# Spreading GpSimd's gathers and scatters over the steps of an attention and the phases of a mixture of experts

## The chip, the cores and the metric

The kernel runs on one core of a Trainium2 chip. The metric is device time in microseconds (us) of one execution. The engines named below are TensorE (PE; its weight loads are shown apart as PEld), VectorE (DVE), ScalarE (ACT), GpSimd (POOL) and SyncE (SP, which only issues DMAs here). Each runs its own stream of instructions in order; between engines, semaphores order the work.

## The reference

Two blocks follow each other: an attention over chunks (4 batches, 8 heads, 768 positions, head dimension 64), and a feed-forward of 8 experts in which each of the 3072 tokens goes to one expert.

```python
for c in range(S // 32):                      # chunks of 32 queries
    q_c   = q[:, :, 32*c : 32*c + 32]
    ctx   = positions max(0, 32*c - 16) .. min(S, 32*c + 40)
    k_full, v_full = [mem_k | k[ctx]], [mem_v | v[ctx]]      # 8 memory rows ahead
    a = softmax(q_c @ k_full.T / sqrt(64))
    out[:, :, chunk] = a @ v_full
x = out.transpose(0, 2, 1, 3).reshape(3072, 512)
logits = x @ w_gate                           # 8 experts
e = argmax(logits);  gate = softmax(logits)[e]
y = gate * (relu(x @ w1[e]) @ w2[e])          # w1[e]: 512 x 1024, w2[e]: 1024 x 512
```

All of it is 32-bit floating point.

## The kernel before

**Attention.** The queries are cut into 32 blocks (`NB`) of 96, three chunks each. One loop, `for i in range(NB + 3)`, holds a software pipeline whose order is written out by hand: step i turns q or k of a later block on PE (L623), computes the scores of block i (L662), takes their exponential on ACT in three instructions (L675), multiplies the exponentials of block i-1 with v (`values`, L686), divides on DVE (L689, L691), turns the result of block i-2 (`turn_xb`, L696, copied by ACT) and computes the gate's logits of block i-3 (L710). SP loads q, k and v some blocks ahead, and from step 6 a quarter of a weight matrix every third step (`fetch_w`). `values` writes its 96 x 528 rows into one of 13 slots of the tile `big`; besides 512 values of x a row holds the gate and the token's number.

**Routing.** Blocks are routed in seven groups, (0,6), (6,12), (12,17), (17,22), (22,27), (27,30), (30,32). Two steps after a group's end `choose` takes the argmax (GpSimd counts the tokens seen of each expert); a step later `label` writes gate and token number into the rows; a step later `rank` works out, with two matmuls and DVE, the row `dest` of each token in a DRAM buffer that is sorted by experts. Then `scatter` (L773) sends each block's 96 rows of 2112 bytes there, an indirect DMA that GpSimd issues. The program has two of them a step. They need only `dest` and the rows; nothing else holds them back.

**Early work.** After group 3, at step 29, GpSimd gathers (L825) the first 256 tokens of expert 0 into `xe2`, followed by a `drain` of its engine; PE turns them (L863) at step 31 and starts their first layer (`early_first`, L869).

**Transition.** After the loop come the last scatters of the group before, `choose` and `label` of the last group, its `rank`, `count_up` (how many tokens each expert has, and the rows to gather), the last two scatters, three memsets on DVE (L1286), the second layer of the early tokens (L1292), and between its halves the gathers of expert 0's and expert 1's tokens, four indirect DMAs of 128 rows each (`fetch_x`).

**Experts.** For each expert `lead` issues three products ahead, then a `Switch` on the number of its tokens takes one of 65 cases. Its width is that number's half, rounded up; an expert too large for one pass is done in two parts (here expert 4). Both layers are matrix products by a scheme of seven products instead of eight (`product`, L1116), which needs sums of quarters of the weights (`sum_weights`, L1092, four of them a layer, DVE) and of x (`sums`, `sum4`). `first_layer` goes through phases: P1 with P2, P6, P7, P5, P4, P3. In each PE makes two products into banks of PSUM, and DVE adds them (L1157, L1165, L1169, L1174, L1176, L1180, L1189), with ReLU on ACT (L1145). Woven in between are the last expert's results, which are turned (`turn_y`, L1039), multiplied by the gate on ACT (L1044) and stored by an indirect DMA (`put_back`, L1050), and the turning of the next expert's x (`turn_x`, L1033, copied by ACT at L1034). GpSimd's program in an expert is: four gathers for expert e + 2 at the beginning, then the four stores. The weight sums for the second layer stand after P7 (two), after P5 (one) and at the end (one). `second_layer` has the same products, with `between` (sums of x and of the next weights) after the first.

Of the kernel before, what the change touches and what calls it, by code (L numbers as in the profile page):

```python
# [24 lines left out]
NB = B * NQB  # L25
# [485 lines left out]
def ordinary(ctx, tc, q, k, v, mem_k, mem_v, moe_w_gate, moe_w1, moe_w2, out, good):  # L511
# [144 lines left out]
    def scores(i):  # L656
        s, (b, qb) = st[i], divmod(i, NQB)
        w0 = window(qb)
        p0 = QB // 2 * (i % 2)
        sc = ps_s.tile([128, H, 128], F32, tag="s", name="sc")  # L660
        for a in range(H // 2):
            mm(  # L662
                sc[:, 2 * a : 2 * a + 2, 0:QB].rearrange("p x (j t) -> p x j t", j=2),
                lhsT=turned[b][:, a, w0 : w0 + WIN],
                rhs=units[i // 2]["qT"][:, a, :, :, p0 : p0 + QB // 2],
                start=True,
                stop=True,
            )
        ex = s["ex"] = apool.tile([128, H, QB], F32, name="ex")
        x = 0 if qb == 0 else 2 if qb == NQB - 1 else 1  # L670
        sc4 = sc[:, :, 0:QB].rearrange("p h (j t) -> p h j t", j=2)
        ex4 = ex.rearrange("p h (j t) -> p h j t", j=2)
        for g in range(3):
            sl = slice(CHUNK // 2 * g, CHUNK // 2 * g + CHUNK // 2)
            nc.scalar.activation(  # L675
                ex4[:, :, :, sl], sc4[:, :, :, sl], AF.Exp, bias=mask[:, 3 * x + g : 3 * x + g + 1], scale=D**-0.5
            )

    def values(i, g, bank):
        s = st[i]  # L680
        if g == 0:
            s["x"] = xr[:, i % NXR, 0:DM]
        o = bank[0:QB, 0 : 4 * (D + 1)].rearrange("p (h d) -> p h d", h=4)
        for j in range(4):
            h = 4 * g + j
            mm(o[:, j], lhsT=s["ex"][:, h], rhs=s["v"][:, h], start=True, stop=True)  # L686

        inv = inv_all[:, i, 4 * g : 4 * g + 4]
        nc.vector.reciprocal(inv, o[:, :, D])  # L689
        x = s["x"].rearrange("p (h d) -> p h d", h=H)  # L690
        nc.vector.tensor_tensor(x[:, 4 * g : 4 * g + 4], o[:, :, 0:D], bc(inv, 2, D), op=OP.mult)  # L691
    def turn_xb(i):
        s = st[i]
        tx = ps_t.tile([128, DM // 128, QB], F32, tag="t", name="tx")
# [73 lines left out]

    scatters = []

    def scatter(t0, t1):
        for t in range(t0, t1):
            i = nc.gpsimd.indirect_dma_start(  # L773
                out=x_dram,
                out_offset=bass.IndirectOffsetOnAxis(ap=dest[:, t : t + 1], axis=0),
                in_=xr[:, t % NXR].bitcast(I32),
                in_offset=None,
                bounds_check=E * XC - 1,
                oob_is_err=False,
            )  # L780
            for j in scatters:
                tc.declare_no_dep(i.ins, j, reason="rows of different tokens")
            scatters.append(i.ins.name)

    def wait_for(i, name):
        tc.add_manual_dep(
# [33 lines left out]

        return rows_of

    def gather(to, which):
        after_scatters(
            nc.gpsimd.indirect_dma_start(  # L825
                out=to.bitcast(I32),
                out_offset=None,
                in_=x_dram,
                in_offset=bass.IndirectOffsetOnAxis(ap=which, axis=0),
                bounds_check=E * XC - 1,  # L830
                oob_is_err=False,
            )
        )

    def need(i, f):
        if 0 <= i < NB:
# [35 lines left out]
    with tc.manual_schedule():  # L872
# [8 lines left out]
        for name, u in ((turn_k, 0), (turn_q, 0), (turn_k, 1)):  # L881
            name(u, 0)
            name(u, 1)
            if name is turn_q:
                turn_mem()
                place_mem(0)
        for i in range(NB + 3):

            u = i // 2 + 1 + i % 2
# [6 lines left out]
            if u < NU:  # L896
                f(u, 0)
            need(i, scores)
            banks = [ps_o.tile([128, 512], F32, tag="o", name="o") for _ in range(2)]
            then = []  # L900
            for g in range(last):
# [10 lines left out]
                values(i - 1, 1, banks[1])  # L912
            if late:
                nc.vector.tensor_copy(*late)
            for f2 in then:
                f2()
            clear(i)
            if u < NU:
                f(u, 1)
            for g in range(last):  # L920
                if i == GROUPS[g][1] + 2:
                    choose(g)
                if i == GROUPS[g][1] + 3:
                    label(g)

            for g in range(last):
                for j in range(2 * (i - GROUPS[g][1] - 4), 2 * (i - GROUPS[g][1] - 4) + 2):
                    t = GROUPS[g][0] + j
                    if GROUPS[g][0] <= t < GROUPS[g][1]:
                        scatter(t, t + 1)  # L930
                        sent = t + 1
            if i == EARLY + 7:
                for g in range(2):
                    gather(xe2[:, g], rows0[:, g : g + 1])
                nc.gpsimd.drain()
            if i == NB - 1:
                early_turn()
            if i >= NB:
# [81 lines left out]
        nc.vector.tensor_scalar(most[:, 0:1], most[:, 0:1], float(XC), None, op0=OP.is_le)  # L1020
        nc.vector.tensor_tensor(good, most[0:1, 0:1], most[0:1, 1:2], op=OP.mult)

    def fetch_x(to, e, k):


        nc.gpsimd.memset(to[:, :, DM].bitcast(I32), SKIP)
        for g in range(4):
            gather(to[:, g], rows[:, e, 2 * k + g // 2, g % 2 : g % 2 + 1])

    def turn_x(x, g):  # L1030
        tx = tiles[g % 2]
# [104 lines left out]
        product(1, banks[2], w, a, 2)  # L1136
        return [turn_y(yTs[(e - 1) % 2], g) for g in (2, 3)] if e else []

    def first_layer(e, hf, backs, turns, new):


        a = halves(xT, KX, hf)
        w, a = weights(e, 0), streams(a, xS[:, :, :, 0:hf])
# [11 lines left out]
        for p in range(2):  # L1155
# [3 lines left out]
                for n in range(4):  # L1159
                    fetch_w(e + 1, 0, n, after=i)  # L1160
            relu(to(0, 0, p))
        for f in backs[:2]:
            f()
        for p in range(2):
            add(T(p), T(p), P(6, p), op=OP.add)  # L1165
        for f in backs[2:]:
            f()
        for p in range(2):
            add(T(2 + p), T(p), P(7, p), op=OP.add)  # L1169
        if new:  # L1170
            sum_weights(e, 1, (5, 6))
        for p in range(2):
            p5 = P(5, p)
            add(to(1, 1, p), T(2 + p), p5, op=OP.add)  # L1174
            relu(to(1, 1, p))
            add(T(p), T(p), p5, op=OP.add)  # L1176
        if new:
            sum_weights(e, 1, (4,))
        for p in range(2):
            add(to(1, 0, p), T(2 + p), P(4, p), op=OP.add)  # L1180
            relu(to(1, 0, p))
        for f in turns[:1]:
            f()
        for p in range(2):
            sums(hh, s, C(p))
            p3 = P(3, p)
            for f in turns[1:2] if p == 0 else turns[2:]:
                f()
            add(to(0, 1, p), T(p), p3, op=OP.add)  # L1189
            relu(to(0, 1, p))  # L1190
        for p in range(2):
            sum4(hh, s, C(p))
        if new:
            sum_weights(e, 1, (7,))

    def second_layer(e, hf, yT, between, last):
        w, a = weights(e, 1), streams(halves(h, KH, hf), hS[:, :, :, 0:hf])
        p1, u2, u3 = (tmp[:, i, :, 0:hf] for i in (0, 4, 5))
        P = lambda i, b: product(i, banks[b], w, a, 0)
        nc.scalar.copy(p1, P(1, 2))  # L1200
        between()
        p4, p5 = P(4, 3), P(5, 4)
        add(u2, p1, P(6, 0), op=OP.add)
        add(u3, u2, P(7, 1), op=OP.add)
        add(yT[:, 2:4, 1, 0:hf], u3, p5, op=OP.add)
        add(u2, u2, p5, op=OP.add)
        add(yT[:, 0:2, 1, 0:hf], u3, p4, op=OP.add)
        add(yT[:, 0:2, 0, 0:hf], p1, P(2, 2), op=OP.add)
        if e + 1 == E and last:
            end_half(yT, tgs[e % 2])  # L1210
        P(3, 5)
# [9 lines left out]
    def expert(e, n, ty):  # L1221
# [8 lines left out]
            backs = [lambda g=g: put_back(*args, g, ty[g - 2]) for g in (2, 3)] + both(put_back, *args)[:2]  # L1230
        yT = yTs[e % 2]
        x = xes[e % 2]
        if len(ps) == 2:
            fetch_x(xe2, e, 1)
        for k, w in enumerate(ps or [0]):
            last = k + 1 >= len(ps)
            tg = tgs[e % 2 if last else 2]
            nc.vector.tensor_copy(tg, x[:, :, DM : DM + 2])
            if k == 0 and e + 2 < E:
                fetch_x(x, e + 2, 0)  # L1240
            x = xes[(e + 1) % 2] if last else xe2
            turns = both(turn_x, x) if not last or e + 1 < E else []
            if w:
                first_layer(e, w // 2, backs, turns, k == 0)
            else:
                for f in backs + turns:
                    f()
                if e + 1 < E:
                    for i in range(4):
                        fetch_w(e + 1, 0, i)  # L1250
# [8 lines left out]
                    sum_weights(e + 1, 0)  # L1259

            if w:
                second_layer(e, w // 2, yT, between, last)
            else:
                between()
                if e + 1 == E:
                    end_half(yT, tg)
            if not last:
# [4 lines left out]
        return {eng.engine: eng.value_load(cases[0:1, c : c + 1], min_val=0, max_val=n - 1) for eng in engines}  # L1272

    with tc.manual_schedule():
        scatter(sent, GROUPS[last][0])
        choose(last)
        label(last)

        for f in range(6, KH):
            early_first(f, banks[f - 2][:, 0])  # L1280
            if f == 6:
                rank(last, banks[2].rearrange("p a b -> p (a b)"))()
                count_up(banks[3])
                scatter(GROUPS[last][0], NB)
        for t in [xes[1]] + yTs:
            nc.vector.memset(t, 0.0)  # L1286
        w2 = ws[0][1].rearrange("p (k n) -> p k n", n=DM)
        engines = (nc.tensor, nc.scalar, nc.vector, nc.gpsimd, nc.sync)
        for g in range(2):
# [1 line left out]
            for f in range(KH):  # L1291
                mm(py, lhsT=h0[:, f, 128 * g : 128 * g + 128], rhs=w2[:, f], start=f == 0, stop=f == KH - 1)  # L1292
            if g == 0:
                fetch_x(xes[0], 0, 0)
                fetch_x(xes[1], 1, 0)
                sum_weights(0, 0)
                index = [loads(engines, e, CASES) for e in range(E)]
                in_range = nc.values_load(good[0:1, 0:1], min_val=0, max_val=1)
                for g2 in range(4):
                    turn_x(xes[0], g2)  # L1300
                sums_of_x()
# [55 lines left out]
```

## Time and profile before

| | |
|---|---|
| median of 3 runs | 599.84 us (596.56 to 600.42) |
| profiled execution | 601.19 us, span 599.4 us |
| mean granted clock of PE | 0.957 |
| busy: PE, DVE, ACT, POOL | 537.7, 323.1, 175.9, 133.6 us |
| chain that ended last | PE 73%, DVE 11%, issue 4%, ACT 4%, another core or an unknown queue 4%, DMA 4% |
| L773 scatters | 32, median 922 ns each |
| L825 gathers | 38, median 1007 ns each |
| L1050 stores by `tg` | 32, mean 1027 ns each |
| L1092 weight sums | 1.22 us each |

The span is the time between the first and the last instruction of the profiled execution; the time of that execution has some 1.8 us more around it. Busy time is the sum of an engine's instructions; for PE it contains the time that they take longer at a lower clock. The granted clock is 1.00 where PE runs at full speed. The chain is followed back from the last instruction to what released each; "another core or an unknown queue" stands for a wait whose end the profile can't put down to a finished instruction or transfer (it is printed as "remote" in the list of waits). A line of a timeline gives start, duration, engine, line of the kernel, operation, output and inputs, and in square brackets how long the engine had been idle and what ended that.

### The profile page before, as it was taken

To read this page: it belongs to the slowest core of one execution; us is meant where nothing else is said; L and a number is where in the kernel's file an instruction comes from. 1 tells how busy PE (TensorE), PEld (TensorE's weight loads), DVE (VectorE), ACT (ScalarE), POOL (GpSimd) and SP (SyncE) were. 2 spreads that over 40 slices of the span, in tenths; PEclk is the share of its full clock that TensorE was granted. 3 is DMA by queue.
4 is the path that set the end of the run, shared out by engine and by line. 5 is a ranking of instruction groups with operands and counts; after the bars stand their busy time and mean duration, and the time that the engine had idled before them with its cause. 6 is when DMAs were issued, how large, how long until landed. Compare 5 with 4: busy or idle time off the path is not lost.

```text
span 599.4 us, 10602 instructions
## 1 busy us (share of the span) xinstructions
PE 537.7 (90%) x3854; PEld 507.8 (85%) x3854; DVE 323.1 (54%) x771; ACT 175.9 (29%) x415; POOL 133.6 (22%) x174
## 2 busy tenths in 40 slices
PE   3999798898899979996999998997999979999994
PEld 3999698788898539986988998986999969998994
DVE  4556355445544563935729728717457195492921
ACT  2556334454442111313023023023050230223201
POOL 3500404030323563022050043041020500301002
PEclk9999889798989979999999998998999979999998
DMA  9999999785403317337054056051032640720002
GB/s 174 179 189 202 246 187 210 182 205 121 113 20 87 89 49 267 120 121 259 6 211 145 4 209 209 17 178 43 1 113 77 246 150 5 252 86 15 14 0 76
DMA packets 81651, 76.07 MB, mean 127 GB/s; under 512 B 39852, under 2 KB 64556, under 8 KB 81456
## 3 DMA queue, kind: packets, MB, share of 16 engines
q1 hardware_dynamic: 72368, 54.54, 37.2%
q0 software_dynamic: 8128, 19.29, 9.4%
q14 instruction: 146, 1.20, 0.6%
q8 instruction: 49, 0.80, 0.6%
q10 hardware_dynamic: 960, 0.24, 0.2%
HBM read 65.04 MB, written 16.45 MB: 136 GB/s over the span
## 4 chain that ended last, share of the span: by engine, by line
PE 73%; DVE 11%; issue 4%; ACT 4%; another core or an unknown queue 4%; DMA 4%; POOL 1%; POOLq 0%; SPq 0%; DVEq 0%; ACTq 0%
PE b L1116 45%; PE sc L662 6%; PE o L686 6%; DVE wT L1092 4%; PE tqk L623 3%; PE o L710 3%; PE t L1039 2%; PE t L1033 2%; PE tx L696 2%; PE b L1292 2%; DMA xe<-x_dram,rows 1%; PE p L869 1%; DMA wg<-in_moe_w_gate_dram 1%; DMA qn<-in_q_dram 1%
## 5 line engine op out<-in xcount | busy, mean ns | idle before, releaser
L1145 ACT ACTIVATE h<-h 128x288 f32<-128x288 f32 (+6 forms) x72 | 33.3, 470 | 126.7 <-DVE h L1174 62.3
L1116 PE MATMUL b<-xT,w 128*128 128x256 f32 (+7 forms) x288 | 58.1, 355 | 4.7 <-issue 4.7
L1116 PEld LDWEIGHTS b<-xT,w 128*128 128x128 f32 x288 | 49.3, 190 | 11.7 <-issue 7.1
L686 PE MATMUL o<-v,ex 128*96 128x65 f32 x512 | 57.1, 257 | 0.8 <-issue 0.8
L1050 POOL DMA_INDIRECT out_dram<-y,tg x32 | 32.9, 1027 | 105.8 <-DMA xe<-x_dram,rows 37.3
L686 PEld LDWEIGHTS o<-v,ex 128*96 128x96 f32 x512 | 53.8, 173 | 0.8 <-issue 0.7
L662 PE MATMUL sc<-qT,kT 128*128 128x192 f32 x256 | 53.3, 356 | 0.0
L689 DVE RECIPROCAL inv_all<-o 96x4 f32<-96x4 f32 x64 | 11.4, 178 | 75.5 <-PE o L686 64.0
L675 ACT ACTIVATE ex<-sc,cst 128x256 f32<-128x256 f32 x96 | 38.4, 471 | 39.6 <-PE sc L662 34.5
L1116 PE MATMUL b<-h,w 128*128 128x144 f32 (+6 forms) x288 | 48.6, 327 | 0.0
L825 POOL DMA_INDIRECT xe<-x_dram,rows x38 | 42.9, 1128 | 18.8 <-issue 7.6
L1116 PEld LDWEIGHTS b<-h,w 128*128 128x128 f32 x288 | 46.1, 210 | 0.6
L662 PEld LDWEIGHTS sc<-qT,kT 128*128 128x128 f32 x256 | 46.2, 211 | 0.0
L1116 PE MATMUL b<-xS,w 128*128 128x144 f32 (+6 forms) x288 | 45.1, 305 | 0.0
L1116 PE MATMUL b<-xS,wT 128*128 128x144 f32 (+6 forms) x288 | 43.9, 306 | 0.0
L1116 PE MATMUL b<-big,w 128*128 128x144 f32 (+6 forms) x288 | 43.9, 306 | 0.0
L1116 PE MATMUL b<-big,wT 128*128 128x144 f32 (+6 forms) x288 | 42.5, 306 | 0.0
L1033 PE MATMUL t<-cst,xe 128*128 128x128 f32 x144 | 24.6, 311 | 19.7 <-ACT xT L1034 15.6
L1156 ACT COPY big<-b 128x288 f32<-128x288 f32 (+6 forms) x18 | 7.6, 420 | 116.9 <-PE b L1116 102.2
L1116 PEld LDWEIGHTS b<-xS,wT 128*128 128x128 f32 x288 | 41.3, 190 | 0.6
L1116 PEld LDWEIGHTS b<-big,w 128*128 128x128 f32 x288 | 41.2, 190 | 0.6
L1116 PEld LDWEIGHTS b<-xS,w 128*128 128x128 f32 x288 | 41.1, 191 | 0.6
(158 smaller groups left out, 890.2 us busy)
## 6 DMA issues: line engine op xcount, KB each, us to landing
w<-in_moe_w_dram SPq DMA_DIRECT2D x64, 512.0 KB
kn<-in_k_dram SPq DMA_DIRECT2D x16, 384.0 KB
qn<-in_q_dram SPq DMA_DIRECT2D x16, 384.0 KB
v<-in_v_dram SPq DMA_DIRECT2D x24, 128.0 KB
v<-in_v_dram SPq DMA_DIRECT2D x24, 112.0 KB
v<-in_v_dram SPq DMA_DIRECT2D x8, 144.0 KB
v<-in_v_dram SPq DMA_DIRECT2D x8, 96.0 KB
xe<-x_dram,rows POOLq DMA_INDIRECT x38
```

Of the source, the lines that this page charges most:

```text
L623: turn(t[:, a], units[u][name][:, 2 * a + x], ident[0:QB, 0:QB])
L662: mm(sc[:, 2 * a : 2 * a + 2, 0:QB].rearrange("p x (j t) -> p x j t", j=2), lhsT=turned[b][:, a, w0 : w0 + WIN], rhs=units[i // 2]["qT"][: ...
L675: nc.scalar.activation(ex4[:, :, :, sl], sc4[:, :, :, sl], AF.Exp, bias=mask[:, 3 * x + g : 3 * x + g + 1], scale=D**-0.5)
L686: mm(o[:, j], lhsT=s["ex"][:, h], rhs=s["v"][:, h], start=True, stop=True)
L696: turn(tx[:, c], s["x"][:, 128 * c : 128 * c + 128], ident[0:QB, 0:QB])
L710: mm(ps, lhsT=s["xT"][:, c], rhs=wg[:, c], start=c == 0, stop=c == DM // 128 - 1)
L825: nc.gpsimd.indirect_dma_start(out=to.bitcast(I32), out_offset=None, in_=x_dram, in_offset=bass.IndirectOffsetOnAxis(ap=which, axis=0), bo ...
L1033: turn(tx[:, c], x[:, g, 128 * c : 128 * c + 128], ident)
L1050: i = nc.gpsimd.indirect_dma_start(out=out, out_offset=bass.IndirectOffsetOnAxis(ap=token.bitcast(I32), axis=0), in_=y, in_offset=None, bo ...
L1092: add(w[i], *of[i], op=OP.subtract)
L1116: mm(bank[:, q, 0:hf], lhsT=w[i][:, c, 128 * (q0 + q) : 128 * (q0 + q) + 128], rhs=a[i][:, c], start=c == 0, stop=c == k - 1,)
L1145: relu = lambda o: nc.scalar.activation(o, o, AF.Relu)
```

## The change

In the attention, groups that are ranked go into a list `due`. The first scatter of a group is issued in the step of its `rank`; then each step below 32 issues one, which waits for the last exponential of that step's scores (`scored`); from step 27 on a second one follows in each step, which waits for the last division of that step (`valued`). What is left after the loop leaves together. The `drain` behind the early gathers is gone.

In the experts a helper `transfers` is called after each of the six phases of the first layer. It issues one gather, which waits for the phase's last add on DVE, and one store. Expert 0 gathers expert 1's tokens in its first four phases (they stood in the transition before); a part that has a second one gathers that in its first four; and the gathers for expert e + 2 take phases five and six, and the adds of P6 and P7 in the second layer. The stores take phases one to four, so the turnings of g = 0 and 1 on PE move from behind P6 to behind P7 and P5. The second layer's weight sums 5, 6, 4 and 7 stand after P1 with P2, after P6, after P7 and at the end. The three memsets of the transition go from DVE, ahead of the second layer of the early tokens, to GpSimd, behind expert 0's gathers.

```diff
-            nc.scalar.activation(
+            done = nc.scalar.activation(
...
+        s["scored"] = done
...
-        nc.vector.tensor_tensor(x[:, 4 * g : 4 * g + 4], o[:, :, 0:D], bc(inv, 2, D), op=OP.mult)
+        s["valued"] = nc.vector.tensor_tensor(x[:, 4 * g : 4 * g + 4], o[:, :, 0:D], bc(inv, 2, D), op=OP.mult)
...
-    def scatter(t0, t1):
+    def scatter(t0, t1, after=None):
...
+            if after is not None:
+                wait_for(i, after.ins.name)
...
+        due = []
+
+        def scatter_next(after=None):
+            t = due.pop(0)
+            scatter(t, t + 1, after)
+
...
+            if due and i < NB:
+                scatter_next(st[i]["scored"])
...
+            if due and i > EARLY + 4:
+                scatter_next(st[i - 1].get("valued") if i - 1 < NB else None)
             for f2 in then:
                 f2()
+            for g in range(last):
+                if i == GROUPS[g][1] + 4:
+                    due.extend(range(*GROUPS[g]))
+                    scatter_next()
...
-            for g in range(last):
-                for j in range(2 * (i - GROUPS[g][1] - 4), 2 * (i - GROUPS[g][1] - 4) + 2):
-                    t = GROUPS[g][0] + j
-                    if GROUPS[g][0] <= t < GROUPS[g][1]:
-                        scatter(t, t + 1)
-                        sent = t + 1
...
-                nc.gpsimd.drain()
...
+        def transfers(after):
+            f = fetch.pop(0) if fetch else None
+            if f:
+                f(after)
+            if backs:
+                backs.pop(0)()
...
-        for f in backs[:2]:
-            f()
+        transfers(i)
+        if new:
+            sum_weights(e, 1, (5,))
         for p in range(2):
-            add(T(p), T(p), P(6, p), op=OP.add)
-        for f in backs[2:]:
-            f()
+            i = add(T(p), T(p), P(6, p), op=OP.add)
+        transfers(i)
+        if new:
+            sum_weights(e, 1, (6,))
         for p in range(2):
-            add(T(2 + p), T(p), P(7, p), op=OP.add)
+            i = add(T(2 + p), T(p), P(7, p), op=OP.add)
+        transfers(i)
         if new:
-            sum_weights(e, 1, (5, 6))
+            sum_weights(e, 1, (4,))
...
-            add(T(p), T(p), p5, op=OP.add)
-        if new:
-            sum_weights(e, 1, (4,))
+            i = add(T(p), T(p), p5, op=OP.add)
+        transfers(i)
...
-        if len(ps) == 2:
-            fetch_x(xe2, e, 1)
+        into = lambda *x: [lambda after=None, g=g: fetch_x(*x, g, after) for g in range(4)]
+
+        fetch = [into(xe2, e, 1)] if len(ps) == 2 else []
+        if e == 0:
+            fetch.append(into(xes[1], 1, 0))
+        more = into(x, e + 2, 0) if e + 2 < E else []
...
-            if k == 0 and e + 2 < E:
-                fetch_x(x, e + 2, 0)
+            soon = fetch.pop(0) if fetch else []
+            later = more if last else []
...
-        for t in [xes[1]] + yTs:
-            nc.vector.memset(t, 0.0)
...
-                fetch_x(xes[0], 0, 0)
-                fetch_x(xes[1], 1, 0)
+                for g2 in range(4):
+                    fetch_x(xes[0], 0, 0, g2)
...
+                for t in [xes[1]] + yTs:
+                    nc.gpsimd.memset(t, 0.0)
```

More of the change, by code (lines that the diff above doesn't have):

```diff
@@ L821, in early_count, with gather @@
         return rows_of
[L823 to L832, printed above, removed]
-        )
+    def gather(to, which, after=None):
+        i = nc.gpsimd.indirect_dma_start(
+            out=to.bitcast(I32),
+            out_offset=None,
+            in_=x_dram,
+            in_offset=bass.IndirectOffsetOnAxis(ap=which, axis=0),
+            bounds_check=E * XC - 1,
+            oob_is_err=False,
+        )
+        after_scatters(i)
+        if after is not None:
+            wait_for(i, after.ins.name)
     def need(i, f):
@@ L1021, in count_up, with fetch_x @@
         nc.vector.tensor_tensor(good, most[0:1, 0:1], most[0:1, 1:2], op=OP.mult)
[L1023 to L1028, printed above, removed]
+    def fetch_x(to, e, k, g, after=None):
+        if g == 0:
+            nc.gpsimd.memset(to[:, :, DM].bitcast(I32), SKIP)
+        gather(to[:, g], rows[:, e, 2 * k + g // 2, g % 2 : g % 2 + 1], after)
     def turn_x(x, g):
@@ L1137, in lead, with first_layer @@
         return [turn_y(yTs[(e - 1) % 2], g) for g in (2, 3)] if e else []
-    def first_layer(e, hf, backs, turns, new):
+    def first_layer(e, hf, backs, turns, new, fetch):
+        fetch, backs = list(fetch), list(backs)
+        def transfers(after):
[4 more added lines that the diff above has]
+                backs.pop(0)()
         a = halves(xT, KX, hf)
@@ L1175, in first_layer @@
             relu(to(1, 1, p))
-            add(T(p), T(p), p5, op=OP.add)
-        if new:
-            sum_weights(e, 1, (4,))
+            i = add(T(p), T(p), p5, op=OP.add)
+        transfers(i)
         for p in range(2):
-            add(to(1, 0, p), T(2 + p), P(4, p), op=OP.add)
+            i = add(to(1, 0, p), T(2 + p), P(4, p), op=OP.add)
             relu(to(1, 0, p))
+        transfers(i)
         for f in turns[:1]:
@@ L1188, in first_layer @@
                 f()
-            add(to(0, 1, p), T(p), p3, op=OP.add)
+            i = add(to(0, 1, p), T(p), p3, op=OP.add)
             relu(to(0, 1, p))
+        transfers(i)
         for p in range(2):
@@ L1194, in first_layer, with second_layer @@
             sum_weights(e, 1, (7,))
-    def second_layer(e, hf, yT, between, last):
+    def second_layer(e, hf, yT, between, last, fetch):
         w, a = weights(e, 1), streams(halves(h, KH, hf), hS[:, :, :, 0:hf])
@@ L1202, in second_layer @@
         p4, p5 = P(4, 3), P(5, 4)
-        add(u2, p1, P(6, 0), op=OP.add)
-        add(u3, u2, P(7, 1), op=OP.add)
+        i = add(u2, p1, P(6, 0), op=OP.add)
+        if fetch:
+            fetch[0](i)
+        i = add(u3, u2, P(7, 1), op=OP.add)
+        if fetch:
+            fetch[1](i)
         add(yT[:, 2:4, 1, 0:hf], u3, p5, op=OP.add)
@@ L1243, in expert @@
             if w:
-                first_layer(e, w // 2, backs, turns, k == 0)
+                first_layer(e, w // 2, backs, turns, k == 0, (soon or [None] * 4) + later[:2])
             else:
-                for f in backs + turns:
-                    f()
+                for g in soon + later[:2] + backs + turns:
+                    g()
                 if e + 1 < E:
@@ L1261, in expert @@
             if w:
-                second_layer(e, w // 2, yT, between, last)
+                second_layer(e, w // 2, yT, between, last, later[2:])
             else:
                 between()
+                for g in later[2:]:
+                    g()
                 if e + 1 == E:
@@ L1274, in ordinary @@
     with tc.manual_schedule():
-        scatter(sent, GROUPS[last][0])
+        while due:
+            scatter_next()
         choose(last)
```

## The prediction

> **What bounds the kernel now.** I read the sums of stages first, since PE is busy 90% of the span and the question is where the other tenth goes and how much of the 90% is only slow clock. Columns: stage, its length, then busy time and instructions of PE, PEld, DVE, ACT and POOL, the granted clock, the DMA share and GB/s.
>
> ```profile
> 41.24:63.32 22.08, 21.76 (x222) 21.65 (x222) 14.05 (x53) 12.06 (x34) 1.69 (x7) 1.00 1.12 197
> 63.32:177.64 114.32, 98.46 (x877) 97.25 (x876) 56.05 (x215) 51.06 (x138) 25.80 (x46) 0.90 0.74 161
> 230.00:575.00 345.00, 322.00 (x2182) 309.48 (x2182) 203.34 (x353) 78.45 (x162) 62.37 (x66) 0.98 0.33 118
> ```
>
> The first stage is five attention steps with no scatters: PE has no gap, 22.08 / 5 = 4.42 us a step. The second is the 20 steps in which GpSimd also scatters: at 4.42 they would need 88.3 us and take 114.3. So **26.0 us** are lost there, partly as idle PE, partly as busy PE at clock 0.90. The third is the experts: 345.0 - 322.0 = **23.0 us** of idle PE, and 2% of clock, some 7 us.
>
> The chain that ended last names the first loss, and GpSimd's timeline stands beside it:
>
> ```profile
> 63.32 1.08 ACT ex L675 x3
> 64.92 6.56 another core or an unknown queue
> 72.64 0.90 PE tx L696 x4
> ```
>
> ```profile
> 62.81 1.09 POOL L773 DMA_INDIRECT x_dram<-big,dest  x1 [6.37 <-DVE dest L765]
> 64.21 0.93 POOL L773 DMA_INDIRECT x_dram<-big,dest  x1 [0.30 <-issue]
> 65.44 0.92 POOL L773 DMA_INDIRECT x_dram<-big,dest  x1 [0.31 <-issue]
> ...
> 69.12 0.92 POOL L773 DMA_INDIRECT x_dram<-big,dest  x1 [0.30 <-issue]
> ```
>
> Six scatters wait only for `dest`, so they leave in one row from 62.81 to 70.04. From 64.92 to 71.48 nobody receives a signal from PE, and signals return 1.4 us after the last scatter. The releaser is "unknown", since the matmuls waited for had ended. The waits show the same, on two engines that wait for PE:
>
> ```profile
> ACT kT L652 <- remote: 13.1, 2, 6.6
> DVE inv_all L689 <- remote: 11.1, 3, 5.7
> ```
>
> The other rows of 6, 5 and 5 scatters (98.11 to 105.18, 128.35 to 134.19, 156.73 to 162.56) do it too, and the clock is near half right after (0.52 over 70 to 80 us). A pair does not:
>
> ```profile
> 183.77 0.95 POOL L773 DMA_INDIRECT x_dram<-big,dest  x1 [4.68 <-DVE inv_all L689]
> 185.03 0.94 POOL L773 DMA_INDIRECT x_dram<-big,dest  x1 [0.30 <-issue]
> ```
>
> PE ran its next 16 matmuls of `early_first` (L869) from 184.76 without a gap, and threes at 188.15 and 194.84 pass as quietly. What blocks is a row longer than three.
>
> In the experts PE's one large wait is the turning of the next expert's x; the DVE timeline of expert 1 shows why:
>
> ```profile
> PE t L1033 <- ACT xT L1034: 15.6, 7, 4.0
> ```
>
> ```profile
> 275.89 0.37 DVE L1169 TENSOR_TENSOR big<-big,b 128x208 f32<-128x208 f32 x1 [2.49 <-remote]
> 276.18 1.22 DVE L1092 TENSOR_TENSOR wT<-w 128x1024 f32<-128x1024 f32 x1
> 277.43 1.23 DVE L1092 TENSOR_TENSOR wT<-w,wT 128x1024 f32<-128x1024 f32 x1
> 278.57 0.36 DVE L1174 TENSOR_TENSOR h<-big,b 128x208 f32<-128x208 f32 x1
> ```
>
> DVE gets P7 late (GpSimd's row of eight transfers ran from 264.48 to 274.64: the same block), and then has two weight sums in a lump ahead of P5's adds.
>
> **The attention: -22 us.** One scatter waits for step i's exp, so the row of six becomes one per step; only the first of a group leaves on its own, and the second about 1.6 us after it (62.81, and exp of step 11 ends at 64.40). Late steps have two. No row is over three until the end, so the block and the half clock go: 26.0 us. Queued behind each waiting scatter on GpSimd are the next scatter, `seen` of a later `choose` and the placing of the memory keys; the slots of `big` are 13 deep, and the slowest scatter of the first group leaves in step 15, so `values` gets its slot some four steps before it writes it. Free, covered by those steps. Two things come back. (1) The loads: the stage moved 161 GB/s x 114.3 us = 18.4 MB; in 92 us that is 200 GB/s, at the upper edge of what the unhindered stage moved (197), but 245 are seen at 62 to 70 us. Nothing to 6 us; I take 2. (2) Each lone scatter may hold PE's signals a little: the nearest rows are the pair above (0) and the two gathers at 176.73 and 178.08 (PE's next start 0.2 to 0.6 us late): 0 to 0.5 us x 22, I take 2, nearer the scatters' own row. -26 + 4 = -22 (-12 to -27). The `drain` that goes had nothing behind it that PE needs: 0; next late there is the landing of the gathers, 3.76 us, which is unchanged.
>
> **Last scatters, memsets, first gathers: -1 us.** Scatter 26 now leaves with 27 to 29 ahead of the last `choose`: one more issue, 0.92 + 0.30 = +1.2 us on the path. Three DVE memsets go from 205.90 to 212.0 to GpSimd behind the gathers that PE waits for, 3 x 1.86 us (L584's 128x2112), with no taker until expert 0: covered by 14 us of L1292. PE starts at 215.33, when the fourth gather has landed:
>
> ```profile
> 210.03 3.92 POOL L825 DMA_INDIRECT xe<-x_dram,rows  x1 [0.30 <-issue]
> ```
>
> The other three took 1.0. If the memset at 210.24 slowed it, 2.9 us are won. The Trainium skill (SBUF — State Buffer, Who interferes with whom) speaks against: a DVE instruction with at most one SBUF input leaves GpSimd alone (outside DVE's two-port modes), so moving memsets wins 0; and three gathers did lie beside memsets at 1.0. What else lay beside the fourth is the sums of weights (211.92 to 216.73), which now come earlier and meet the same gathers. Between 0 and -2.9 I take -2.2, because four gathers and sums now overlap from the start, but GpSimd is done sooner. With +1.2: -1 (-5 to +2).
>
> **The experts: -16 us.** One gather and one store a phase: no row of eight, so no block. One sum a phase: a phase is 1.96 us of PE, DVE's share 0.92 + 1.22 = 2.14, so DVE falls back 0.2 a phase, 0.6 in three, instead of 2 x 1.22 at once. DVE's sum of work is unchanged. Of the 15.6 us at L1033 I take 12 away; of the block inside the first layers (PE gaps of 0.84 and 0.48 us at 274 to 276, and the like in two or three other experts) 3; of half clock after these waits (3.4 us stretches at 282, 371 and 415, each worth half) 5, less 2 for those that other idle time causes.
>
> Here a rule speaks against the change: DMA: Bandwidth & Descriptors, Rules for kernel authors, wants a DMA issued early and awaited late. Gathers for e + 2 have a whole expert, 0. But expert 0 now gathers `xes[1]` in its own first four phases, and the two-part expert its second part: the fourth gather leaves after P5's adds, some 3.9 us (two phases) ahead of its `turn_x`, and needs 3.76 us from issue to landing by the pair at 178.08. By the rule that is a wait of up to the full 5 us a place; by the row it is 0 to 1.2. I take 1 us x 2. So 12 + 3 + 3 - 2 = 16 (-6 to -24).
>
> **Sum.** 601.19 of the profiled run (599.4 span + 1.8) - 22 - 1 - 16 = 562; that run lay 1.35 above the median, so 561 against 599.84.
>
> **The rivals.** *Loads become the bound* (0.12): the block hid that attention waits for q, k and v. For: 197 GB/s at DMA share 1.12 before the first row. Against: PE never waited for a load after the start, and 245 GB/s are seen. At 5 us a step in steps 11 to 20 attention gives -16, the weights that queue behind them cost 4 of the experts' 16: 601.2 - 16 - 1 - 12 - 1.35 = 571.
> *The experts stay* (0.11): spread sums are still all on DVE, and each now stands between an add and the next bank's release. For: 2.14 against 1.96. Only attention's gain and the transition's: 601.2 - 22 - 1 - 1.35 = 577.
> *Nothing changes* (0.05): the waits are met already when GpSimd gets there, as it would be if it ran steps behind; against it, the row starts within step 10. 600.
> *A scatter blocks PE whatever its spacing* (0.12), the slower side: what was one block of six becomes six. Price: 0.92 + 1.2 us after it = 2.1 us x 32 = 67, less 26, no gain in the experts since gathers do the same: about 640. It decides from 26 / 32 = 0.8 us each. Against it, the pair and the threes at 183 to 198 us, which cost nothing.
>
> **Chances.** The forecast 0.60, so faster by over 1% (6 us, about what a measurement of this kernel can tell from no change) 0.60 + 0.12 + 0.11 = 0.83, within 1% 0.05, slower 0.12. Low end: -27 - 5 - 24 = -56, so 544; high end: -12 + 2 - 6 = -16, so 584, widened by 6 to take in the spread of the rival at 577: 590.
>
> **What would show it.** Scatters alone, 4 us apart; steps 11 to 30 in 90 to 95 us at clock near 1.00; no "unknown queue" in the chain. In the experts L1092 one at a time between adds, L1033's wait under 5 us. Wrong if exp's steps stay over 5 us with gaps after each scatter, or if ACT or PE waits for q, k, v loads.

## The result, and the profile after

The changed kernel takes 548.96 us (median of 4 runs, 548.51 to 549.4) against 598.2 us for the kernel before (median of 4, 592.46 to 600.42: the three runs of the table above and one more): a ratio of 0.919, with a 95% interval from 0.9121 to 0.926. The profiled execution has a span of 547.1 us instead of 599.4, 52.3 us less, and a mean granted clock of 0.992 instead of 0.957. The forecast was 561 us, 39 less than its base; the direction and the mechanism of the attention hold; the size was too small, above all in the experts.

The page of the changed kernel, its row of the granted clock in 40 slices and its chain by engine:

```profile
PEclk9999999999999999999999999999999999999997
PE 81%; DVE 6%; issue 5%; DMA 4%; ACT 1%; POOL 1%; POOLq 1%; SPq 0%; ACTq 0%; DVEq 0%
```

The slices below 9 are gone but for the last, and so is the chain's entry "another core or an unknown queue", which was 4% of the span before. PE's share of the chain rose from 73% to 81%, DVE's fell from 11% to 6%.

The sums by stage, of the changed kernel (columns as in the prediction): five steps without scatters, the 20 steps with them, the transition up to expert 0's first product, the experts, and the end.

```profile
41.23:63.32 22.09, 21.77 (x222) 21.65 (x222) 14.05 (x53) 12.06 (x33) 1.68 (x7) 1.00 1.07 183
63.32:151.98 88.66, 87.09 (x877) 86.46 (x876) 56.41 (x215) 50.75 (x139) 25.77 (x46) 1.00 1.02 212
151.98:198.12 46.14, 41.04 (x212) 28.99 (x211) 19.95 (x86) 10.04 (x23) 23.38 (x26) 0.96 0.26 76
198.12:522.00 323.88, 316.72 (x2206) 305.91 (x2205) 203.58 (x354) 80.28 (x164) 72.67 (x73) 1.00 0.37 128
522.00:547.10 25.10, 16.21 (x85) 14.33 (x83) 4.53 (x7) 2.54 (x4) 3.93 (x4) 0.88 0.12 46
```

The same cuts in the kernel before, for the three stages that the prediction did not show with these limits:

```profile
177.64:225.47 47.83, 42.16 (x212) 29.67 (x211) 25.00 (x88) 10.14 (x23) 24.83 (x28) 0.93 0.28 82
225.47:574.40 348.93, 325.93 (x2200) 312.93 (x2200) 203.96 (x355) 79.93 (x164) 63.49 (x68) 0.98 0.33 117
574.40:599.40 25.00, 17.29 (x90) 15.31 (x88) 4.54 (x7) 2.53 (x4) 3.94 (x4) 0.93 0.12 46
```

| stage | before | after | difference | forecast |
|---|---|---|---|---|
| up to step 11 | 63.32 | 63.32 | 0 | 0 |
| steps 11 to 30 | 114.32 | 88.66 | -25.66 | -22 |
| transition | 47.83 | 46.14 | -1.69 | -1 |
| experts | 348.93 | 323.88 | -25.05 | -16 |
| end | 25.00 | 25.10 | +0.10 | 0 |

They add to -52.3, the difference of the spans.

**The attention.** GpSimd's timeline of the changed kernel at the first group of scatters:

```profile
62.82 1.09 POOL L775 DMA_INDIRECT x_dram<-big,dest  x1 [6.38 <-DVE dest L767]
64.80 0.93 POOL L775 DMA_INDIRECT x_dram<-big,dest  x1 [0.89 <-ACT ex L675]
69.72 0.92 POOL L775 DMA_INDIRECT x_dram<-big,dest  x1 [3.99 <-ACT ex L675]
...
73.57 0.93 POOL L775 DMA_INDIRECT x_dram<-big,dest  x1 [2.52 <-ACT ex L675]
78.33 0.92 POOL L775 DMA_INDIRECT x_dram<-big,dest  x1 [3.83 <-ACT ex L675]
```

The releaser of the four scatters shown after the first is the exponential of a step, and from the second on they start 3.9 to 4.9 us apart. The stage has 1.57 us of idle PE (88.66 - 87.09) instead of 15.86 (114.32 - 98.46), which is 14.3 us less; the clock is 1.00 instead of 0.90, and PE is busy for 11.4 us less (98.46 - 87.09) with the same 877 matmuls. So over half of the gain is idle time, and the rest is clock.

**The experts.** PE's waits in the changed kernel, from 198 to 522 us:

```profile
PE b L1128 <- issue: 5.4, 8, 0.9
PE t L1045 <- DMA xe<-x_dram,rows: 1.4, 1, 1.4
PE t L1045 <- ACT xT L1046: 0.2, 1, 0.2
PE t L1045 <- issue: 0.2, 1, 0.2
```

(The columns are us in total, how often, the longest.) The wait for ACT's copy of the turned x, 15.6 us before, is 0.2. DVE's timeline in the first layer of expert 1 shows what stands ahead of it now (L1104 is the line of the weight sums, L1092 before):

```profile
238.74 1.22 DVE L1104 TENSOR_TENSOR wT<-w 128x1024 f32<-128x1024 f32 x1
239.87 0.67 DVE L1188 TENSOR_TENSOR big<-big,b 128x208 f32<-128x208 f32 x2
240.46 1.22 DVE L1104 TENSOR_TENSOR wT<-w,wT 128x1024 f32<-128x1024 f32 x1
241.59 0.74 DVE L1193 TENSOR_TENSOR big<-big,b 128x208 f32<-128x208 f32 x2
242.24 1.22 DVE L1104 TENSOR_TENSOR wT<-w,wT 128x1024 f32<-128x1024 f32 x1
```

No two sums follow each other in a first layer, and no add among these waits for a signal that comes late.

### The profile page after: what moved, and what is told of

The parts are those of the page before. It is cut to its first block, busy times and chain, and to the rows that moved or that the text cites. A ratio compares the mean times of both kernels' runs of the same rounds, so it can differ in the third digit from the quotient of the medians.

```text
span 547.1 us, 10646 instructions
## 1 busy us (share of the span) xinstructions
PE 514.7 (94%) x3854; PEld 488.1 (89%) x3854; DVE 318.0 (58%) x768; ACT 175.8 (32%) x415; POOL 141.3 (26%) x177
## 4 chain that ended last, share of the span: by engine, by line
PE 81%; DVE 6%; issue 5%; DMA 4%; ACT 1%; POOL 1%; POOLq 1%; SPq 0%; ACTq 0%; DVEq 0%
PE b L1128 53%; PE sc L662 6%; PE o L687 6%; PE tqk L623 3%; PE o L712 3%; PE t L1045 2%; PE t L1051 2%; DMA xe<-x_dram,rows 2%; PE p L874 2%; PE b L1327 2%; PE tx L698 1%; DMA wg<-in_moe_w_gate_dram 1%; DMA qn<-in_q_dram 1%; DVE wT L1104 1%; DVE qT L631 1%
## 5 line engine op out<-in xcount | busy, mean ns | idle before, releaser
L1062 POOL DMA_INDIRECT out_dram<-y,tg x32 | 35.3, 1102 | 136.8 <-DMA out_dram<-y,tg 55.1
L687 PE MATMUL o<-v,ex 128*96 128x65 f32 x512 | 54.0, 248 | 0.0
L687 PEld LDWEIGHTS o<-v,ex 128*96 128x96 f32 x512 | 50.6, 165 | 0.0
L662 PE MATMUL sc<-qT,kT 128*128 128x192 f32 x256 | 49.2, 336 | 0.0
L775 POOL DMA_INDIRECT x_dram<-big,dest x32 | 29.7, 927 | 69.2 <-ACT ex L675 34.3
L1128 PE MATMUL b<-h,w 128*128 128x144 f32 (+6 forms) x288 | 43.9, 306 | 0.0
L662 PEld LDWEIGHTS sc<-qT,kT 128*128 128x128 f32 x256 | 42.2, 195 | 0.0
L1128 PEld LDWEIGHTS b<-h,w 128*128 128x128 f32 x288 | 41.1, 190 | 0.6
L1128 PEld LDWEIGHTS b<-big,wT 128*128 128x128 f32 x288 | 40.8, 190 | 0.6
```

The source lines that it names most:

```text
L662: mm(sc[:, 2 * a : 2 * a + 2, 0:QB].rearrange("p x (j t) -> p x j t", j=2), lhsT=turned[b][:, a, w0 : w0 + WIN], rhs=units[i // 2]["qT"][: ...
L775: i = nc.gpsimd.indirect_dma_start(out=x_dram, out_offset=bass.IndirectOffsetOnAxis(ap=dest[:, t : t + 1], axis=0), in_=xr[:, t % NXR].bit ...
L1062: i = nc.gpsimd.indirect_dma_start(out=out, out_offset=bass.IndirectOffsetOnAxis(ap=token.bitcast(I32), axis=0), in_=y, in_offset=None, bo ...
L1128: mm(bank[:, q, 0:hf], lhsT=w[i][:, c, 128 * (q0 + q) : 128 * (q0 + q) + 128], rhs=a[i][:, c], start=c == 0, stop=c == k - 1,)
```

## The experiments

No kernel besides these two was run. So what follows rests on two traces and on what differs inside them; no cause was taken out by itself. Three questions would each have needed kernels of their own:

- How much of the experts' 25 us is due to the spread transfers and how much to the spread weight sums. It would take the attention's part of the change alone, that part with the sums spread, and the changed kernel with the sums back at their places. If the sums do all of it, the last of these loses some 25 us; if the transfers do, it loses nothing. (What the traces say of it stands in the next section.)
- From what length of a row of scatters PE's signals are held. It would take the changed kernel with two, three, four or five scatters in one row, rows two steps apart, and one with rows of six half scatters of 48 tokens, which tells the number of transfers from the number of tokens.
- What the `drain` and the place of the three memsets are worth by themselves: each put back alone.

None of these was tried. What is said below on these questions is argued from the two traces, and not shown by experiment.

What the traces do tell apart are the rivals, since each named a stage and a size.

*A scatter blocks PE whatever its spacing* expected 2.1 us for each, on balance about 640 us. The 20 steps with scatters take 88.66 us, while the pace of the five steps without them gives 88.3. The scatters of these steps together cost 0.3 us more than none at all. The rival falls.

*Loads become the bound* expected 5 us a step. The stage moved 212 GB/s at 4.43 us a step, had 1.57 us of idle PE in all, and neither PE nor ACT nor DVE waited for a DMA in it. It falls.

*The experts stay* expected 577 us and no gain after the transition; the gain there is 25 us. *Nothing changes* expected 600 us and rows of scatters as before; the timeline above shows one at a time. Both fall.

## Why the prediction was right or wrong

**The attention: right in mechanism, two terms of 2 us each that measured near 0.** The step was -26.0, plus 2 for loads and 2 for lone scatters that hold PE's signals a little. Both together measured 88.66 - 88.3 = 0.3 us. The estimate of 200 GB/s for the loads was near (212 measured), but this rate was no limit: before the first scatter it is 183 at the same pace. For the lone scatters I took a middle between a pair of scatters that cost nothing and a pair of gathers that cost 0.2 to 0.6 us; the scatters' own row was the one to take.

One reading of the trace before was not exact. The prediction says that nobody receives a signal from PE from 64.92 to 71.48. DVE received one at 70.06, just as the sixth scatter's issue ended:

```profile
70.06 0.18 DVE L689 RECIPROCAL inv_all<-o 96x4 f32<-96x4 f32 x1 [4.43 <-remote]
71.50 1.09 ACT L652 COPY kT<-tqk 64x192 f32<-64x192 f32 x4 [6.58 <-remote]
```

The matmuls that DVE waited for had ended at 65.68 (64.81 + 0.87), so this signal was 4.4 us late; the others came together at 71.5. The loss and its cause are read the same.

**Last scatters, memsets, first gathers: -1.69 instead of -1, near by luck, since the terms were wrong.** I put 1.2 us on the path for scatter 26 leaving with 27 to 29. Ahead of the last `choose` of the changed kernel there are three scatters (169.12, 170.34 and 171.57), as many as before (194.84, 196.07, 197.29); scatter 26 left at 164.89, in the step before. So this term is 0. For the gathers I took -2.2. From the end of the row count (start of L1021 at 205.03, now L1033 at 179.30) to PE's turning of the fourth gather it was 10.30 us and is 9.63, a gain of 0.7. GpSimd's four gathers of expert 0's tokens in the changed kernel:

```profile
180.35 1.49 POOL L828 DMA_INDIRECT xe<-x_dram,rows  x1 [2.68 <-DVE good L1033]
182.14 1.01 POOL L828 DMA_INDIRECT xe<-x_dram,rows  x1 [0.30 <-issue]
183.46 2.00 POOL L828 DMA_INDIRECT xe<-x_dram,rows  x1 [0.30 <-issue]
185.76 0.99 POOL L828 DMA_INDIRECT xe<-x_dram,rows  x1 [0.30 <-issue]
```

And DVE beside them, the weight sums for expert 0, which start at once now that no memset is ahead of them:

```profile
179.71 1.23 DVE L1104 TENSOR_TENSOR wT<-w 128x1024 f32<-128x1024 f32 x1 [0.26 <-issue]
180.97 2.49 DVE L1104 TENSOR_TENSOR wT<-w,wT 128x1024 f32<-128x1024 f32 x2
183.37 1.22 DVE L1104 TENSOR_TENSOR w<-w 128x1024 f32<-128x1024 f32 x1
```

The slow fourth gather (3.92 us) is gone, but the first and the third are slow instead, and the sums lie beside these. They lie beside the second too, which took 1.01. Nor do the sums account for the fourth gather before. DVE had, beside its issue from 210.03 to 213.95:

```profile
210.24 1.76 DVE L1286 MEMSET yT<- 128x2048 f32 x1 [0.38 <-issue]
211.92 1.16 DVE L1092 TENSOR_TENSOR wT<-w 128x1024 f32<-128x1024 f32 x1
```

When the first sum began, that issue had lasted 1.9 us, and the other three took 1.0 in all. So the sums can't have begun the delay, and only the memset lay beside its first part; but three gathers had memsets beside them as well and took 1.0. The prediction's reading, that the memsets had not slowed the fourth gather, is neither confirmed nor refuted, and the cause of that delay stays open.

The rest of the 1.69 us lies in steps at half clock. The turning of the fourth gather takes 0.63 us instead of 1.09, and the half of L1292 (L1327 now) behind it 8.56 instead of 9.04. The stretch at clock 0.50 there was 6.83 us long (213.85 to 220.68, with 5.35 us of busy PE) and is 3.41 (189.69 to 193.10).

**The experts: -25 instead of -16.** Idle PE fell from 348.93 - 325.93 = 23.0 us to 323.88 - 316.72 = 7.2, so by 15.8, where the step had 12 + 3 - 2 = 13. Its terms: 12 us of the wait at L1033 were to go; 15.4 went (15.6 to 0.2). The block inside the first layers was put at 3; PE's gaps there (at 274 to 276, 406 to 408 and 480) were 2.5 us and are gone. The other gaps put down to "issue", at the beginning of each first layer, went from 4.7 to 5.4. Late gathers were put at 1 us in two places; it is 1.4 in one, the two-part expert, and nothing in expert 0. So the prediction's rule to issue a DMA early gave the right direction there, and the row of the pair at 178.08, 0 to 1.2 us, the nearer size; the "full 5 us" were an estimate, and no trace shows them.

The term that was sized wrong is the clock. I gave 3 us to it; busy PE fell by 325.93 - 316.72 = 9.2 us for the same matmuls. The stage had four stretches at half clock:

```profile
282.11:285.52 3.41, 3.10 (x15) 3.11 (x16) 2.60 (x9) 2.57 (x6) 0.00 (x0) 0.50 0.36 133
370.86:374.27 3.41, 3.41 (x14) 3.38 (x13) 3.26 (x8) 2.01 (x4) 2.80 (x3) 0.50 0.74 279
415.23:418.64 3.41, 3.29 (x15) 3.29 (x16) 3.20 (x9) 2.41 (x6) 0.00 (x0) 0.50 0.02 5
486.91:493.74 6.83, 5.93 (x24) 5.93 (x25) 6.59 (x13) 3.34 (x7) 0.00 (x0) 0.50 0.18 68
```

PE is busy for 15.73 us of them, and half of that is 7.9 us, most of the 9.2. I counted the first three and missed the fourth, the longest, and then took 2 us off for other idle time. None of the four is left in the changed kernel, whose clock is 1.00 in this stage. The stage itself had the figure: 2% of 345 us is 7, which I had read and not used.

**What the wait at L1033 came from.** The prediction shows the block (the row of transfers that holds PE's signals) in expert 1, puts it at 3 us for PE's gaps there and in two or three other experts, and sets the sums spread one to a phase against the lump of two for the wait at L1033. The list of waits seems to agree, since it has a wait for a "remote" signal in the first layers of experts 1 and 4 only. But that name is not a sure sign: where other matmuls ended shortly before the late signal comes, the profile puts the wait down to PE. A surer sign is the time from the end of a product to the add that needs it. In expert 5, which has no "remote" wait, GpSimd's row of eight lasted from 468.92 to 479.16, and PE and DVE have:

```profile
473.57 2.34 PE L1116 MATMUL b<-xS,w 128*128 128x160 f32 x16
480.38 0.49 DVE L1169 TENSOR_TENSOR big<-big,b 128x320 f32<-128x320 f32 x1 [2.40 <-PE b L1116]
```

The matmuls of P7 end at 475.91, and the add of its second product starts 4.5 us later, though DVE had been idle for 2.4. The same phase of the changed kernel, 0.04 us from end to add:

```profile
428.22 2.34 PE L1128 MATMUL b<-xS,w 128*128 128x160 f32 x16
430.60 0.49 DVE L1193 TENSOR_TENSOR big<-big,b 128x320 f32<-128x320 f32 x1 [0.15 <-PE b L1128]
```

All first layers before that have the two sums in a lump and an x to turn behind them:

| expert | transfers in GpSimd's row | P7 ends | its second add starts | late by | PE's wait at L1033 |
|---|---|---|---|---|---|
| 0 | 4 | 235.75 | 236.40 | 0.7 | 1.1 |
| 1 | 8 | 270.67 | 275.89 | 5.2 | 3.4 |
| 2 | 8 | 312.95 | 315.54 | 2.6 | 1.3 |
| 3 | 8 | 359.70 | 362.45 | 2.8 | 2.0 |
| 4, first part | 8 | 404.16 | 408.19 | 4.0 | 3.0 |
| 5 | 8 | 475.91 | 480.38 | 4.5 | 4.0 |
| 6 | 4 | 519.23 | 519.94 | 0.7 | 0.8 |

So every row of eight held PE's signals, with or without the name "remote", and 13.7 of the 15.6 us lie in these five experts. Experts 0 and 4 have products of the same width and the same lump of sums; the row of four goes with a wait of 1.1 us, the row of eight with 3.0. This speaks for the rows of transfers as the larger cause and for some 1 us an expert, as an estimate from experts 0 and 6, that the lump and a short row cost together. It does not prove it, since transfers and sums moved at once in every expert.

**One step is weaker than I put it.** I wrote that what blocks is a row longer than three. In the two-part expert of the changed kernel, gathers and stores, which wait in the same queue, still leave as a row of eight:

```profile
360.43 1.22 POOL L828 DMA_INDIRECT xe<-x_dram,rows  x1 [7.18 <-DVE h L1179]
361.96 1.61 POOL L1062 DMA_INDIRECT out_dram<-y,tg  x1 [0.30 <-issue]
363.87 1.64 POOL L828 DMA_INDIRECT xe<-x_dram,rows  x1 [0.31 <-issue]
...
371.45 1.03 POOL L1062 DMA_INDIRECT out_dram<-y,tg  x1 [0.30 <-issue]
```

Each after the first follows 0.3 us behind the one before. Yet P7 ends at 363.00 there and its add starts at 363.04; only near the row's end is an add late, the last of P3, by 0.9 us at most. What differs from the rows of eight before is the pace, (371.45 - 360.43) / 7 = 1.57 us against (273.65 - 264.48) / 7 = 1.31 in expert 1 and up to 1.36 in the others, and the traffic, 198 GB/s from 360 to 373 us against 268 to 309 in the five stretches before. Traffic alone is not the condition, since the row of scatters at 156.73, which did block, stands in a stretch of 128 GB/s. Before, rows of three scatters blocked nothing, rows of four at the experts' pace made an add up to 0.9 us late, and all rows of five, six and eight blocked. That fits a row that has to be both long and dense; one row at a slower pace does not show it, and the mechanism stays open.

## What to carry to other kernels

When engines that have nothing to do with a DMA stop together, look for a dense row of indirect DMAs on GpSimd in the same microseconds, and give each a wait on something that happens once a step; transfers with slack lose nothing by it. Do not go by the releaser's name alone: set the start of an instruction against the end of the work that it needs. Work that an engine has in a lump ahead of adds that free a bank for PE can be put one piece to a phase in the same change; what that is worth by itself was not shown here. And price the clock from all of a stage's stretches at a lower clock, or from its granted clock and its length, rather than from the stretches that one can explain.

## What the runs showed of the hardware that was not expected

Rows of eight gathers and stores held PE's signals in every expert that had one, by 2.6 to 5.2 us (the table above), as rows of scatters did in the attention; the list of waits names it in two of these experts only.

The issue of an indirect DMA on GpSimd often takes longer beside DVE's weight sums, whose two inputs both lie in SBUF. In the changed kernel from 169 us on, the 55 indirect DMAs that overlap no sum take 1.01 us in the mean and 1.28 at most, and the 24 that do take 1.30 in the mean, up to 2.00. Before, from 170 us on, 81 without overlap took 1.00 in the mean and 1.24 at most, and the five with it 1.0 to 3.9. (Worked out by laying the timelines of the two engines over each other.) In both together, 12 of the 29 with overlap took over 1.3 us and none of the 136 without. Why the other 17 were not slowed is not shown, and the slowest of all, 3.92 us, was slow before a sum began. It cost little here, since GpSimd is busy for only 26% of the span, but at the first gathers PE waits for it.
